# Mixture-of-depths behind ABC attention: row sums in staggered lanes, v's rows stored twice, softmax by halves, and an order from modelled times

## Chip, core and metric

One core of one Trainium2 chip. The metric is the device time of one execution in microseconds, input and output in the chip's memory; the median of several runs counts.

## The reference, cut to what matters

```python
# q, k, v: (8, 8, 576, 64) batch, head, token, width; phi: (8, 8, 576, 32)
a = softmax(phi, axis=2)                        # over the 576 tokens
k_m = einsum('bhsm,bhsd->bhmd', a, k)
v_m = einsum('bhsm,bhsd->bhmd', a, v)
attn = softmax(q @ k_m.transpose(0, 1, 3, 2) / 8)
x = (attn @ v_m), heads side by side            # (8, 576, 512)
scores = einsum('bsd,d->bs', x, w_gate)
out = x.copy()
for b in range(8):                              # the 128 tokens of highest score
    top = argpartition(-scores[b], 128)[:128]
    h = relu(x[b, top] @ w1)                    # 512 -> 1024
    out[b, top] += sigmoid(scores[b, top]) * (h @ w2)
```

The choice of the 128 tokens hangs on close scores, so the softmax is worked out in pieces with a second, small part, and v and a are split into a rounded part ("hi", fp32r) and what is left ("lo").

## The kernel before

A *pair* is a batch and one of its two groups of four heads (4 x 32 memory slots = 128 partitions). The kernel runs through stages, each written as Python generators that take turns; what a generator issues between two `yield`s stands together on each engine, and each engine works in that order.

- **Softmax** (`softmax`, L191 to L277): one batch at a time, both groups side by side in tiles of 128x1152 (`ph`, `num`, `den`, `rl`, `lin`). VectorE does nearly all passes, ScalarE the linear steps and the exponentials (`act`, L187), GpSimd two additions (L223, L267).
- **`split_v`** (L279): ScalarE rounds v to `vhi`, GpSimd subtracts (L288), and GpSimd stores both parts to the tensor `vparts` in HBM (L291).
- **`keys`** (L297): TensorE transposes a (L306), ScalarE copies it to `aS`, GpSimd takes lo (L312) and stores hi and lo twice each to `aparts` (L316); TensorE sums k into `k_m` (L321) and turns it (L331).
- **`values(st)`** (L337): the row sums v_m of four batches at once, one matmul per token and batch (L363). Each batch has 32 partitions (two copies x two parts x eight heads): `v_rows` holds v's rows, `a_rows` a's rows on the diagonal of heads, zeros elsewhere, so that 32 x 64 of v against 32 x 256 of a gives all eight heads. 18 chunks of 32 tokens; a chunk is loaded by eight DMAs of 128 KB for v (L345, 16 partitions side by side each) and eight of 64 KB for a (L350, every eighth partition), all on SP, into one of two buffers.
- **`attention_and_ffn(b)`**: `centre`, `scores` (q against `kT`, L423; exp), `normal` (L404 to L410), `attend` (L475, L478, the gate's scores on VectorE L459 to L464, the store of x, L486), `rank` (the place of each token by comparing, L499 to L530), `gather` (L537 to L551) and `ffn` (L575 w1, L583 w2, store L590).

The order of the stages:

```python
finish(beside(turns([batch(b) for b in range(half)], 8), chain(...split_v...), 1))
...
finish(beside(beside(turns([batch(b) for b in range(half, B)], 8), sums, 2), splits, 1))
...
finish(beside(turns([attention_and_ffn(b) for b in range(SET)], 14, 3), sums, 1))
finish(sums)
finish(turns([attention_and_ffn(b) for b in range(SET, B)], 14, 3))
```

The first `sums` is `values(0)`, beside the softmax of batches 4 to 7; the second is `values(1)`, beside the attention of batches 0 to 3. Buffers of the softmax are given back before the attention's are taken.

Of the kernel before, what the change touches and what calls it, by code (L numbers as in the profile page):

```python
# [20 lines left out]
P = 128  # L21
NC = 6

# [18 lines left out]
NC_T = 6  # L42
# [3 lines left out]
def kernel(  # L46
# [10 lines left out]
    vparts: bass.AP,  # L57
    aparts: bass.AP,
# [9 lines left out]
    NG = phiT.shape[2]  # L68
# [5 lines left out]
    SET = 4  # L74
    T = 32
    NCH = S // T
    scale = 1.0 / Dh ** 0.5
    out_flat = out.rearrange("b s d -> (b s) d")
    pieces = [(n0, min(2 * P, S - n0)) for n0 in range(0, S, 2 * P)]

    nt = -(-capacity // P)
    ranks = [(t * capacity // nt, (t + 1) * capacity // nt) for t in range(nt)]
    assert all(2 <= r1 - r0 <= P for r0, r1 in ranks) and capacity < S

    const = ctx.enter_context(tc.tile_pool(name="const", bufs=1))
    rows = ctx.enter_context(tc.tile_pool(name="rows", bufs=1))
    accp = ctx.enter_context(tc.tile_pool(name="accp", bufs=1, space=PSUM))
    pss = ctx.enter_context(tc.tile_pool(name="pss", bufs=4, space=PSUM))
    first = ExitStack()
    io = first.enter_context(tc.tile_pool(name="io", bufs=2))  # L90
    ex = first.enter_context(tc.tile_pool(name="ex", bufs=2))

    def bank(shape, dtype=F32, name="bank"):
        return pss.tile(list(shape), dtype, tag="bank", name=name)

    phis, ks, qs, vbs = {}, {}, {}, {}

    def load_phi(b):
        phis[b] = io.tile([P, NG, S], F32, name="ph", bufs=3)
        nc.sync.dma_start(out=phis[b], in_=phiT[b])  # L100

    def load_k(b, g):
        ks[b, g] = io.tile([PT, NC, NPR * Dh], F32, name="kb")
        nc.sync.dma_start(out=ks[b, g], in_=k[b, g])

    def load_v(b, g):
        vbs[b, g] = io.tile([P, S * Dh * NPR // P], F32, name="vb")
        nc.sync.dma_start(out=vbs[b, g], in_=v[b, g])

    def load_q(b, i):  # L110
        n0, n = pieces[i]
        qs[b, i] = step.tile([P, NPR, 2 * P], F32, name="qb", bufs=3)
        nc.sync.dma_start(out=qs[b, i][:, :, :n], in_=qT[b, :, :, n0:n0 + n])

    load_phi(0)
    load_v(0, 0)

    ident = const.tile([P, P], F32, name="ident")
    make_identity(nc, ident)

    v_rows = [rows.tile([P, (T + 1) * Dh], F32R, name=f"v_rows{i}") for i in range(2)]
    a_rows = [rows.tile([P, H, T, M], F32R, name=f"a_rows{i}") for i in range(2)]

    kT = [const.tile([P, P], F32, name=f"kT{i}") for i in range(B)]
    v_m = [const.tile([P, P], F32, name=f"v_m{i}") for i in range(B)]
    zs = [const.tile([P, NG, NPR * Dh], F32, name=f"zs{i}") for i in range(2)]

    wg = const.tile([P, D], F32, name="wg")
    iota_r = const.tile([P, capacity], F32, name="iota_r")
    place = const.tile([P, NT], F32, name="place")  # L130
    later = const.tile([P, S], F32, name="later")
    blocks = const.tile([P, P], F32, name="blocks")
    centre_m = const.tile([P, P], F32, name="centre_m")
    means = const.tile([P, NPR, P], F32, name="means")
# [6 lines left out]
    def zero_rows():
        for t in v_rows + a_rows:
            nc.gpsimd.memset(t.bitcast(F32), 0.0)

    def early_consts():
# [6 lines left out]
        nc.vector.scalar_tensor_tensor(out=centre_m, in0=blocks, scalar=-1.0 / M, in1=ident,  # L152
                                       op0=ALU.mult, op1=ALU.add)

    def late_consts():
        nc.sync.dma_start(out=wg, in_=bass.AP(
            tensor=w_gate.tensor, offset=w_gate.offset,
            ap=[[0, P]] + [list(x) for x in w_gate.ap]))
        for t in zs:
            nc.gpsimd.memset(t, 0.0)  # L160
# [15 lines left out]
    def constant(value):  # L176
        t = const.tile([P, 1], F32, name=f"c{len(biases)}")
        nc.gpsimd.memset(t, value)
        return t

    biases = {}
    Q_SHIFT = (127 - 14) * 2.0 ** 23
    for x in (EXP_P[1] * Y0, EXP_Q[1], SQ_B, 1.0, Y0, Q_SHIFT, Y0_BIAS, 1e-9):
        biases[x] = constant(x)

    def act(dst, src, s=1.0, c=0.0, func=AF.Identity):
        nc.scalar.activation(dst, src, func, bias=biases[c] if c else 0.0, scale=s)  # L187
# [531 lines left out]
```

## Time and profile before

| | us |
|---|---|
| median of 3 runs | 1087.49 (1077.97 to 1087.73) |
| the profiled execution | 1083.98 |
| its span, first to last instruction | 1082.3 |

Busy shares of engines are of the span, or of the stretch that a row names. A DMA share of 1 is all 16 DMA engines at work. PEclk is the granted clock of TensorE as a share of 2.4 GHz. "Idle before" is the time for which an engine had nothing to do ahead of a group of instructions, with what ended it.

### The profile page before, as it was taken

To read this page: it belongs to the slowest core of one execution; us is meant where nothing else is said; L and a number is where in the kernel's file an instruction comes from. 1 tells how busy PE (TensorE), PEld (TensorE's weight loads), DVE (VectorE), ACT (ScalarE), POOL (GpSimd) and SP (SyncE) were. 2 spreads that over 40 slices of the span, in tenths; PEclk is the share of its full clock that TensorE was granted. 3 is DMA by queue.
4 is the path that set the end of the run, shared out by engine and by line. 5 is a ranking of instruction groups with operands and counts; after the bars stand their busy time and mean duration, and the time that the engine had idled before them with its cause. 6 is when DMAs were issued, how large, how long until landed. Compare 5 with 4: busy or idle time off the path is not lost. (4 is left out here: it accounts for less than half of the span.)

```text
span 1082.3 us, 17052 instructions
## 1 busy us (share of the span) xinstructions
PE 545.8 (50%) x7162; PEld 426.8 (39%) x7162; DVE 415.5 (38%) x550; ACT 316.1 (29%) x457; POOL 226.1 (21%) x218
## 2 busy tenths in 40 slices
PE   0001201214444456441212767777879877698876
PEld 0000101113444445431111646665656654466555
DVE  7958598545343410347600022011103421434340
ACT  1425345141223100134310413112224305554410
POOL 8536433262324120121530000000000000000000
PEclk9999999957677778765555887688878888697887
DMA  2366621649889889831349899888931121321010
GB/s 87 133 237 237 182 84 34 168 131 239 231 242 237 208 201 159 189 94 53 104 147 241 140 188 158 145 166 151 166 89 54 59 69 54 97 87 61 29 60 13
DMA packets 54147, 146.70 MB, mean 136 GB/s; under 512 B 16560, under 2 KB 24752, under 8 KB 49456
## 3 DMA queue, kind: packets, MB, share of 16 engines
q1 hardware_dynamic: 43056, 103.59, 42.5%
q0 software_dynamic: 11008, 41.95, 11.8%
q8 instruction: 59, 0.97, 0.4%
q14 instruction: 24, 0.20, 0.1%
HBM read 96.21 MB, written 49.28 MB: 134 GB/s over the span
## 5 line engine op out<-in xcount | busy, mean ns | idle before, releaser
L363 PE MATMUL acc<-a_rows,v_rows 32*128 32x256 f32 x4608 | 210.9, 345 | 214.6 <-DMA a_rows<-aparts 180.8
L363 PEld LDWEIGHTS acc<-a_rows,v_rows 32*128 32x128 f32 x4608 | 194.6, 248 | 233.2 <-issue 166.4
L321 PE MATMUL bank<-kb,aS 96*32 96x64 f32 x768 | 24.1, 296 | 130.2 <-ACT aS L308 119.0
L306 PE MATMUL bank<-ident,ph 128*96 128x128 f32 x96 | 23.4, 400 | 102.8 <-DVE ph L271 95.0
L321 PEld LDWEIGHTS bank<-kb,aS 96*32 96x32 f32 x768 | 18.7, 156 | 137.0 <-ACT aS L308 124.0
L575 PE MATMUL bank<-xeT,w_sb 128*128 128x128 f32 x512 | 69.5, 297 | 1.5 <-ACT xeT L568 1.5
L575 PEld LDWEIGHTS bank<-xeT,w_sb 128*128 128x128 f32 x512 | 65.4, 208 | 7.0 <-issue 4.0
L208 DVE SCALAR_TENSOR_TENSOR ph<-q,ph 128x1152 f32<-128x1152 int16 x16 | 28.3, 1767 | 102.5 <-ACT q L187 102.2
L590 POOL DMA_INDIRECT out<-ye,idx x8 | 8.0, 995 | 285.0 <-DVE more L509 208.3
L459 DVE TENSOR_TENSOR prod<-xj,wg 128x1024 f32<-128x1024 f32 (+1 forms) x24 | 25.1, 1044 | 107.3 <-ACT xj L482 107.2
L410 DVE SCALAR_TENSOR_TENSOR eT<-es,rd 128x512 f32<-128x512 f32 (+1 forms) x24 | 13.4, 559 | 136.6 <-ACT rd L408 136.6
L288 POOL TENSOR_TENSOR vb<-vb,vhi 128x1152 f32<-128x1152 f32 x16 | 44.0, 2752 | 92.3 <-ACT vhi L283 92.3
L583 PE MATMUL bank<-w_sb,hT 128*128 128x512 f32 x128 | 62.7, 626 | 0.0
L475 PE MATMUL bank<-zs,eT 128*128 128x256 f32 (+1 forms) x160 | 58.7, 502 | 0.0
L306 PEld LDWEIGHTS bank<-ident,ph 128*96 128x96 f32 x96 | 16.1, 195 | 106.6 <-DVE ph L271 64.5
L551 POOL DMA_INDIRECT xe<-out,idx x8 | 7.9, 989 | 215.5 <-DMA v_rows<-vparts 143.4
L312 POOL TENSOR_TENSOR alo<-aS,ahi 96x768 f32<-96x768 f32 x16 | 33.1, 2066 | 89.3 <-ACT ahi L310 89.3
L283 ACT ACTIVATE vhi<-vb 128x1152 fp32r<-128x1152 f32 x16 | 18.6, 1160 | 110.5 <-DMA vb<-in_v 78.7
L308 ACT ACTIVATE aS<-bank 96x384 f32<-96x384 f32 x32 | 15.0, 476 | 108.0 <-PE bank L306 107.8
L427 ACT ACTIVATE es<-bank 128x256 f32<-128x256 f32 (+1 forms) x48 | 13.2, 324 | 105.6 <-PE bank L423 105.5
L223 POOL TENSOR_TENSOR den<-den,lin 128x1152 f32<-128x1152 f32 x8 | 25.8, 3230 | 85.2 <-DVE den L222 50.3
L509 DVE SCALAR_TENSOR_TENSOR more<-row,tg,later 128x576 bf16<-128x576 f32 (+4 forms) x40 | 20.4, 546 | 59.9 <-ACT row L503 59.9
(121 smaller groups left out, 989.8 us busy)
## 6 DMA issues: line engine op xcount, KB each, us to landing
v_rows<-vparts SPq DMA_DIRECT2D x288, 128.0 KB, 6.3
a_rows<-aparts SPq DMA_DIRECT2D x288, 64.0 KB, 3.9
vb<-in_v SPq DMA_DIRECT2D x16, 576.0 KB, 4.5
vparts<-vb POOLq DMA_DIRECT2D x16, 576.0 KB, 3.6
vparts<-vhi POOLq DMA_DIRECT2D x16, 576.0 KB, 5.1
kb<-in_k SPq DMA_DIRECT2D x16, 576.0 KB, 5.7
aparts<-alo POOLq DMA_DIRECT2D x32, 288.0 KB, 4.1
aparts<-ahi POOLq DMA_DIRECT2D x32, 288.0 KB, 4.8
```

The lines of the kernel that those rows point to most:

```text
L208: stt(out=r, in0=q, scalar=-ln2, in1=r, op0=ALU.mult, op1=ALU.add)
L223: nc.gpsimd.tensor_add(den, den, lin)
L288: nc.gpsimd.tensor_sub(vb, vb, hi.bitcast(F32))
L306: nc.tensor.transpose(out=tp[:, c], in_=a[:, c0 + c], identity=ident)
L312: nc.gpsimd.tensor_sub(lo, aS, hi.bitcast(F32))
L321: nc.tensor.matmul(out=km[r * M:(r + 1) * M], lhsT=aS[:, r, c], rhs=kb[:, c, r * Dh:(r + 1) * Dh], start=(c == 0), stop=(c == NC - 1), ski ...
L363: nc.tensor.matmul(out=accs[bb][:, :H * M].rearrange("p (h m) -> p h m", m=M), lhsT=vr[p, s * Dh:s * Dh + P], rhs=ar[p, :, s], start=(ch = ...
L459: nc.vector.tensor_mul(prod[:n, :cols], x, wg[:n].unsqueeze(1).to_broadcast([n, cols, D]))
L475: nc.tensor.matmul(out=o[:n, g * NPR * Dh:(g + 1) * NPR * Dh], lhsT=eT[:, g, tok:tok + n], rhs=z[:, g], start=(g == 0), stop=False, skip_g ...
L509: nc.vector.scalar_tensor_tensor(out=more[c][:n], in0=row[:n, c * P:], scalar=tg[:n, c, 1:2], in1=later[:n, :S - c * P], op0=ALU.is_gt, op ...
L575: nc.tensor.matmul(out=ps[:, f, :n], lhsT=w1_sb[:, d, (f0 + f) * P:(f0 + f + 1) * P], rhs=xeT[:, d, :n], start=(d == 0), stop=(d == KD - 1 ...
L583: nc.tensor.matmul(out=ps[:n], lhsT=hT[:, f, :n], rhs=w2_sb[:, f], start=(f == 0), stop=(f == KF - 1))
```

## The change

**Lanes.** The row sums of all batches become one sequence of 99 steps of 16 tokens. Lane g (partitions 32g to 32g+31) takes batch g and then batch g+4, and begins nine steps (144 tokens) behind lane g-1. One, two or three lanes are active in 18 steps each, four in 45. A lane's 32 partitions are two parts of v x two of a x four heads x two head groups; v's row stands in the half of the columns that belongs to its group (zeros in the other), so a matmul is 32 x 128 against 32 x 128 and its 128 output partitions hold both groups.

**Rows.** `v_lanes` holds each part of v twice (four stores of 576 KB a pair instead of two). A step is loaded by two DMAs for v (every second partition of the active lanes, 64 KB per lane) and eight for a (8 KB per lane), given in turn to SP or GpSimd: 501 to SP, 489 to GpSimd. There are three row buffers.

**Softmax by halves.** One pair at a time, tiles of 128x576, two pairs in turn. The additions of L223 and L267 and both subtractions go from GpSimd to VectorE.

**Order by a time model.** Every step of every job says which engine it needs, for how long by the author's figures, and which buffers. `Plan.run` keeps a clock per engine and one for DMA, and again and again issues the step with the earliest modelled start, with a bonus for waiting and a malus by job.

```diff
+LANES, T, LAG = 4, 16, 9
+class Plan:
+    RATE = 300.0
+    BIAS = 0.4
+    AGE = 0.3
+    QUEUES = {"Q": ("SP", "POOL"), "QA": ("SP", "POOL", "ACT")}
...
+                engine = min(self.QUEUES.get(engine, (engine,)), key=lambda x: self.free[x])
+                start = max(ready, self.free[engine])
+                key = start + self.BIAS * job[0] - self.AGE * (start - ready)
+                if best is None or key < best[0]:
+                    best = key, start, job, engine, us, names, kb
...
+            end = start + us
+            self.free[engine] = end
+            job[1] = self.now = end + (0.15 if job[3][0] not in self.QUEUES else -0.65)
+            if kb:
+                self.dma = max(self.dma, end + 1.0) + kb / self.RATE
+                self.now = self.dma + 0.9
...
-        nc.gpsimd.tensor_add(den, den, lin)
+        yield "DVE", 0.76
+        tt(out=den, in0=den, in1=lin, op=ALU.add)
...
-        nc.gpsimd.tensor_add(r, r, dl)
+        tt(out=e, in0=e, in1=dl, op=ALU.add)
...
-        nc.gpsimd.tensor_sub(lo, aS, hi.bitcast(F32))
+            lo, = yield "DVE", 0.95, ("alo",)
+            nc.vector.tensor_sub(lo, aS, hi.bitcast(F32))
...
+    def store_v(b, g, w, src, pool, item):
+        yield "POOL", 1.4, (), 1152
+        for alpha in range(2):
+            r0 = ((b % LANES) * 4 + alpha * 2 + w) * NPR
+            dst = v_lanes[g, r0:r0 + NPR, col(b):col(b) + S]
+            nc.gpsimd.dma_start(out=dst.rearrange("h (j s) d -> j h (s d)", j=P // NPR), in_=src)
...
+    def split(b, g, vb):
+        hi, = yield "ACT", 1.16, ("vhi",)
+        nc.scalar.activation(hi, vb, AF.Copy)
+        yield "DVE", 1.36
+        nc.vector.tensor_sub(vb, vb, hi.bitcast(F32))
...
+    def load_v(j, u, eng):
+        on = active(j)
+        g0, g1 = on[0], on[-1] + 1
+        eng.dma_start(out=turn[j][0].bitcast(F32)[32 * g0 + u:32 * g1:NG, :, u],
+                      in_=v_lanes[u, 16 * g0:16 * g1, j * T:(j + 1) * T])
+    def load_a(j, hs, eng):
...
+            eng.dma_start(
+                out=ar[32 * g0 + r * NG + u:32 * g1:H, r].rearrange("p s m -> p (s m)"),
+                in_=a_lanes[r, u, 4 * g0:4 * g1, j * T:(j + 1) * T].rearrange("i s m -> i (s m)"))
...
+    def sums():
+        for j in range(steps):
+            yield "wait", ("rows", j)
+            on = active(j)
+            for s0 in range(0, T, T // 2):
+                yield "PE", 0.12 * T / 2
+                vr, ar = turn[j]
+                for s in range(s0, s0 + T // 2):
+                    for g in on:
...
+                            out=accs[g][:, x * P:(x + 1) * P].rearrange("p (r m) -> p r m", m=M),
+                            lhsT=vr[p, s].rearrange("p u d -> p (u d)"), rhs=ar[p, :, s],
...
+    plan.add(load_phi(pairs), 0)
+    plan.add(constants(), 1)
+    plan.add(split_v(pairs), 1)
+    plan.add(softmax(pairs[0::2]), 0)
+    plan.add(softmax(pairs[1::2]), 0)
+    plan.add(load_k(pairs), 1)
+    plan.add(keys(pairs), 0)
+    plan.add(load_rows(), 0)
+    plan.add(sums(), 0)
+    plan.add(attention(range(0, B, 2)), 1)
+    plan.add(attention(range(1, B, 2)), 1)
+    plan.add(ffn(range(B)), 2)
+    plan.run()
```

How the order moves, at three places. A row is a line, an operation, what it writes and reads, its size, and a count where it stands several times in a row. First, TensorE where the row sums begin. Before, they follow the keys of batch 3 (L331 turns its k_m), and the four batches of the stage alternate:

```order
L306 MATMUL bank<-ident,ph 96x128 x6
L321 MATMUL bank<-kb,aS 32x64 x24
L331 MATMUL bank<-centre_m,kms 128x128
L363 MATMUL acc_858<-a_rows_86,v_rows_84 128x256
L363 MATMUL acc_859<-a_rows_86,v_rows_84 128x256
L363 MATMUL acc_860<-a_rows_86,v_rows_84 128x256
L363 MATMUL acc_861<-a_rows_86,v_rows_84 128x256
```

Now, the same place: they follow the keys of batch 0 (L413, L426), with the transposes of batch 1 (L395) in between:

```order
L413 MATMUL bank_115<-kb_144,aS_145 32x64 x24
L426 MATMUL bank_116<-centre_m,kms_148 128x128
L525 MATMUL acc_104<-a_rows_109,v_rows_108 128x128 x16
L395 MATMUL bank_117<-ident,ph_120 96x128 x3
L525 MATMUL acc_104<-a_rows_111,v_rows_110 128x128 x8
L395 MATMUL bank_114<-ident,ph_120 96x128 x3
```

The sums begin three batches earlier and run with one lane at first. 1,888 of the 4,608 stand ahead of the last key matmuls (L413) of batch 7, in steps 0 to 42.

Second, TensorE at the last row sums. Before, the transposes of v_m (L374) follow, and the ranking of batch 1 (L520):

```order
L363 MATMUL acc_4179<-a_rows_87,v_rows_85 128x256
L363 MATMUL acc_4180<-a_rows_87,v_rows_85 128x256
L363 MATMUL acc_4181<-a_rows_87,v_rows_85 128x256
L363 MATMUL acc_4182<-a_rows_87,v_rows_85 128x256
L374 MATMUL bank<-ident,turned 128x64 x4
L520 LDWEIGHTS more_7026
L520 MATMUL bank<-ones_113,more_7026 128x1
```

Now, the same place, with the last lane alone (acc_107) between the attention of batch 4 (L650, L653) and an FFN (L761 is its transpose, L540 turns the last v_m):

```order
L525 MATMUL acc_107<-a_rows_111,v_rows_110 128x128 x16
L650 MATMUL bank_115<-z_152,eT_158 64x256 x2
L653 LDWEIGHTS ones_91
L653 MATMUL bank_115<-hb_154,ones_91 64x512
L525 MATMUL acc_107<-a_rows_113,v_rows_112 128x128 x16
L761 MATMUL bank_114<-ident,w_137 128x128 x4
L540 MATMUL bank_117<-ident,turned_151 128x128
L691 MATMUL bank_116<-ident,tg_98 128x128 x4
```

Behind the last sum stand 192 of the 256 matmuls with w1, 48 of 64 with w2, 30 of 80 of L650, 48 of 128 of q against kT, and the ranking and gathering of four batches.

Third, the queues of the row loads. Before, SP alone, at the first chunks of a stage (`v_rows_84` and `v_rows_85` are the two buffers):

```order
L156 DMA wg<-in_w_gate 128x512
L100 DMA ph<-in_phiT 128x1152
L345 DMA v_rows_84<-vparts 16x2048 x8
L350 DMA a_rows_86<-aparts 16x1024 x8
L345 DMA v_rows_85<-vparts 16x2048 x8
L350 DMA a_rows_87<-aparts 16x1024 x8
```

Now, GpSimd where four lanes become active, with the stores of v and a (`vhi`, `vb`, `ahi`, `alo`) between the loads; SP has the other half of each step:

```order
L451 DMA v_lanes<-vhi_143 32x4x1152 x2
L451 DMA v_lanes<-vb_141 32x4x1152 x2
L479 DMA v_rows_112<-v_lanes 48x16x64
L487 DMA a_rows_113<-a_lanes 12x512 x4
L441 DMA a_lanes<-ahi_146 96x4x192 x2
L441 DMA a_lanes<-alo_147 96x4x192 x2
L479 DMA v_rows_108<-v_lanes 64x16x64
L487 DMA a_rows_109<-a_lanes 16x512 x4
```

One load of v and about four of a per step stand on each queue, and GpSimd's stand behind stores that wait for VectorE.

## Rows read from the trace of the kernel before

**Rows 1.** The page's first lines: span, and each engine's busy time, share and instructions

```profile
span 1082.3 us, 17052 instructions
PE 545.8 (50%) x7162; PEld 426.8 (39%) x7162; DVE 415.5 (38%) x550; ACT 316.1 (29%) x457; POOL 226.1 (21%) x218
```

**Rows 2.** Busy time by stage: stretch, length, then each engine, granted clock, DMA share, GB/s

```profile
0.00:62.00 62.00, 0.00 (x0) 0.00 (x0) 50.41 (x31) 20.00 (x19) 39.88 (x40) 1.00 0.34 124
62.00:239.00 177.00, 28.18 (x440) 20.65 (x440) 116.70 (x103) 68.97 (x89) 79.33 (x76) 0.93 0.48 150
239.00:490.00 251.00, 118.93 (x2532) 111.11 (x2532) 92.09 (x79) 51.30 (x65) 61.46 (x49) 0.72 0.83 200
490.00:560.00 70.00, 15.31 (x228) 11.82 (x228) 37.46 (x43) 25.39 (x38) 27.97 (x25) 0.52 0.28 80
560.00:801.00 241.00, 157.91 (x2661) 128.28 (x2665) 29.28 (x71) 44.86 (x70) 2.32 (x4) 0.76 0.87 170
801.00:1083.00 282.00, 225.51 (x1309) 154.94 (x1301) 89.56 (x226) 105.58 (x177) 15.17 (x26) 0.81 0.17 56
```

**Rows 3.** Groups by line: the row sums, busy, mean ns, idle time before, releasers

```profile
L363 PE MATMUL acc<-a_rows,v_rows 32*128 32x256 f32 x4608 | 210.9, 345 | 214.6 <-DMA a_rows<-aparts 180.8 <-DMA v_rows<-vparts 24.6 <-DMA vb<-in_v 7.4
```

**Rows 4.** Timeline of TensorE around 750 us: start, length, instructions

```profile
749.18 1.23 PE L363 MATMUL acc<-a_rows,v_rows 32*128 32x256 f32 x32
750.33 2.05 PE L575 MATMUL bank<-xeT,w_sb 128*128 128x128 f32 x16
752.31 1.23 PE L363 MATMUL acc<-a_rows,v_rows 32*128 32x256 f32 x32
```

**Rows 5.** Timeline of the first 60 us: VectorE and GpSimd

```profile
6.32 15.25 DVE L202 TENSOR_SCALAR ph<-ph,mx 128x576 f32<-128x576 f32 x2
13.91 6.93 POOL L143 MEMSET a_rows<- 128x8192 f32 x1
...
34.55 1.36 DVE L222 SCALAR_TENSOR_TENSOR den<-rl,den 128x1152 f32<-128x1152 f32 x1
...
36.06 3.58 POOL L223 TENSOR_TENSOR den<-den,lin 128x1152 f32<-128x1152 f32 x1 [7.81 <-DVE den L222]
37.21 3.65 DVE L225 SCALAR_TENSOR_TENSOR num<-rl,num 128x1152 f32<-128x1152 f32 x1
...
54.61 0.75 DVE L246 SCALAR_TENSOR_TENSOR ph<-num,two_q 128x576 f32<-128x576 f32 x1
```

**Rows 6.** DMA: bytes in all, and issues by tile, KB each, median us to landing

```profile
DMA packets 54147, 146.70 MB, mean 136 GB/s; under 512 B 16560, under 2 KB 24752, under 8 KB 49456
...
v_rows<-vparts SPq DMA_DIRECT2D x288, 128.0 KB, 6.3
a_rows<-aparts SPq DMA_DIRECT2D x288, 64.0 KB, 3.9
...
vparts<-vb POOLq DMA_DIRECT2D x16, 576.0 KB, 3.6
```

**Rows 7.** Issue of DMAs: SP's a loads, GpSimd's stores (min/median/max), and eight a loads

```profile
L350 SPq DMA_DIRECT2D a_rows<-aparts x288: 471/536/1907, 227.2 to 790.6; - x144
...
L316 POOL DMA_DIRECT2D aparts<-alo x32: 677/677/720, 105.4 to 556.4; - x32
...
602.25 7.06 SPq L350 DMA_DIRECT2D a_rows<-aparts  x8
```

**Rows 8.** Groups of TensorE from 801 us on: busy us, mean ns, idle before

```profile
L575 PE MATMUL bank<-xeT,w_sb 128*128 128x128 f32 x448 | 59.8, 294 | 1.5 <-ACT xeT L568 1.5
L583 PE MATMUL bank<-w_sb,hT 128*128 128x512 f32 x112 | 52.2, 603 | 0.0
L475 PE MATMUL bank<-zs,eT 128*128 128x256 f32 (+1 forms) x120 | 44.6, 509 | 0.0
```

More of the change, by code (lines that the diff above doesn't have):

```diff
@@ L1 @@
 from contextlib import ExitStack
-from itertools import chain
 import concourse.bass as bass
@@ L73 @@
     KD, KF = D // P, F // P
-    SET = 4
-    T = 32
-    NCH = S // T
+    half = S // 2
     scale = 1.0 / Dh ** 0.5
     out_flat = out.rearrange("b s d -> (b s) d")
[L79 to L86, printed above, removed]
@@ L141, in zero_rows, with sb, several @@
[L141 to L145, printed above, removed]
+    per = S // T
+    steps = (B // LANES) * per + (LANES - 1) * LAG
+    assert capacity <= P and capacity < S and S % T == 0
+    mem = ctx.enter_context(tc.tile_pool(name="mem", bufs=1))
+    psum = ctx.enter_context(tc.tile_pool(name="psum", bufs=1, space=PSUM))
+    def sb(shape, dtype=F32, name="sb"):
+        return mem.tile(list(shape), dtype, name=name)
+    def several(n, shape, dtype=F32, name="sb"):
+        return [sb(shape, dtype, f"{name}{i}") for i in range(n)]
@@ new lines, in load_k, with softmax, chain_of @@
+    def load_k(pairs):
+        for b, g in pairs:
+            yield "wait", ("half", b, g)
+            kb, = yield "SP", 0.6, ("kb",), 576
+            ks[b, g] = kb
+            nc.sync.dma_start(out=kb, in_=k[b, g])
+            signal(("k", b, g))
+    def softmax(pairs):
+        for b, g in pairs:
+            yield "wait", ("phi", b, g)
+            yield from chain_of(b, g)
+    def chain_of(b, g):
+        r = phis.pop((b, g))
+        sm, i16 = yield "DVE", 1.31, ("sm", "i")
+        mx, den_s, rcp, top, low = (sm[:, x:x + 1] for x in range(5))
+        q, rh = i16[:, 0], i16[:, 1]
+        nc.vector.tensor_reduce(mx, r, axis=AX.X, op=ALU.max)
+        signal(("begun", b, g))
+        yield "DVE", 0.46
+        nc.vector.tensor_scalar(out=r, in0=r, scalar1=mx, scalar2=EXP_LOWEST,
+                                op0=ALU.subtract, op1=ALU.max)
+        yield "ACT", 0.65
@@ L615, in turns @@
-    def turns(jobs, lag, width=2):
-        jobs, live, since = list(jobs), [], lag
-        while jobs or live:
-            if jobs and len(live) < width and since >= lag:
-                live.append(jobs.pop(0))
-                since = 0
-            since += 1
-            for job in list(live):
-                if next(job, live) is live:
-                    live.remove(job)
-                else:
-                    yield
-    def beside(main, other, n):
-        for _ in main:
-            for _ in range(n):
-                next(other, None)
-            yield
@@ L636, in batch @@
-    def batch(b):
-        if b + 1 < B:
-            load_phi(b + 1)
-        yield from softmax(b)
-    early_consts()
-    zero_rows()
-    half = B // 2
-    finish(beside(turns([batch(b) for b in range(half)], 8),
-                  chain(*[split_v(b) for b in range(half)]), 1))
-    splits = chain(*[split_v(b) for b in range(half, B)])
-    late_consts()
-    sums = values(0)
-    finish(beside(beside(turns([batch(b) for b in range(half, B)], 8), sums, 2), splits, 1))
-    finish(splits)
@@ L664 @@
-    sums = values(1)
-    finish(beside(turns([attention_and_ffn(b) for b in range(SET)], 14, 3), sums, 1))
-    finish(sums)
-    finish(turns([attention_and_ffn(b) for b in range(SET, B)], 14, 3))
-    ps = bank([1, B, len(pieces)])
-    nc.tensor.matmul(out=ps.rearrange("p b i -> p (b i)"), lhsT=ones,
-                     rhs=good.rearrange("p b i -> p (b i)"), start=True, stop=True)
-    sums_ok = work.tile([1, B, len(pieces)], F32, name="sums_ok")
-    for i, (n0, n) in enumerate(pieces):
-        nc.vector.tensor_single_scalar(sums_ok[:, :, i], ps[:, :, i], H * n - 0.5, op=ALU.is_gt)
```

988 lines of the change are left out of this document (556 added, 432 removed).

## The prediction

> **What bounds the kernel now.** I read the page's shares first: TensorE is busy half of the 1082.3 us span and no engine more [rows 1]. So the time is lost between engines, and the table by stage says where [rows 2]. From 0 to 239 us VectorE is busy 50.4 and 116.7 us, TensorE hardly: softmax of four batches. From 239 to 490 us the row sums of batches 0 to 3 run beside the second softmax, and the DMA share is 0.83. From 490 to 560 us the rest of that softmax runs nearly alone. From 560 to 801 us the sums of batches 4 to 7 run beside the first attentions, DMA share 0.87, TensorE busy 158 of 241 us. From 801 us TensorE is busy 225.5 of 282 us and the DMA share is 0.17. The bound changes four times. That DMA is the limit of the two row stages is seen at the sums' own line: 214.6 us of idle time ahead of it, 180.8 of them ended by a landing of a_rows [rows 3].
>
> **The change, part by part.** The stages become one program, and its engine orders have three stretches. I price each by the resource that ends it.
>
> *DMA.* The kernel moves 146.7 MB today; 288 loads of 128 KB (37.7 MB) and 288 of 64 KB (18.9 MB) are rows [rows 6]. v's two parts are stored twice now, another 32 stores of 576 KB, 18.9 MB, so 165.6 MB. At what rate? Outside the row stages a full share is worth 56/0.17 = 329 GB/s (801 to 1083 us) [rows 2]. The stage from 560 us moved 170 GB/s x 241 us = 41.0 MB in 0.87 x 241 = 210 us of full share; 28.3 MB were rows, the other 12.7 MB at 329 take 39 us, so the rows ran at 28.3/171 = 165 GB/s. A v load filled 16 partitions side by side; now it takes every second partition of all lanes. No row shows that form: its bounds are 165 and 329 GB/s. I take 329 for v, whose spread over the partitions now resembles the other tiles' loads, and 165 for a, whose loads shrink.
>
> *VectorE.* Four jobs leave GpSimd for it (the two subtractions, the two softmax additions). A pass over half the columns takes 0.75 us (L246), a whole undisturbed one 1.36 us (L222) [rows 5]. A half needs 20 passes (15.0 us), v's subtraction at 1.36, a's (96x768, between these two) at 0.93, a maximum and a clamp (0.7 and 0.5) and small ones (0.9): about 19.5 us, 16 times is 312 us. What it gets in return: beside a GpSimd addition a VectorE pass took 3.65 us instead of 1.36, and two clamps took 15.25 us beside the clearing of a_rows [rows 5]. GpSimd has no such work after its start now.
>
> *Row sums.* 4,608 matmuls stay, but 128 columns wide instead of 256, because two head groups share the 128 output partitions. Warm, 32 of the old ones lie 1.15 us apart from the next piece (749.18 to 750.33), so four lanes' step costs 144 ns [rows 4]. Where columns alone decide it falls to 72, where weights or issue decide it stays 144. I take 110 ns per token step, between the ends because the trace does not separate weights from columns, and give steps with fewer than four lanes the same price. The Trainium skill (TensorE: Matmul & The Clock Gate, "Wait - 56ns, not 53.3ns?") says that starts of matmuls never come closer than about 25 ns, however narrow. By that rule 2,720 sums of the second stretch take an estimated 68 us instead of my 99, and the time would be some 40 us shorter; no run here shows it yet.
>
> *First stretch, to the last keys.* 1,888 of the 4,608 sums (41%) stand ahead of the last key matmuls on TensorE. So DMA moves phi, k, v (23.5 MB), the stores (56.6 MB), the weights (4.4 MB) and 41% of the rows (23.2 MB: 15.5 of v, 7.7 of a). That is 84.5/329 = 257 us, 47 us and 47 us: 351 us. The row stages never passed a share of 0.87 [rows 2], so 351/0.87 = 403 us. VectorE needs 312/0.92 + 22 us to begin = 361 us, less; GpSimd and SP issue some 630 and 610 DMAs in all, at 0.68 and 0.54 us [rows 7] nowhere near. I take 405; ends are 361 (VectorE alone) and 457 (all rows at 165).
>
> *Second stretch, to the last sum.* Attention work on TensorE: from 801 us seven FFNs ran (448 of 512 and 112 of 128 records), 59.8 + 52.2 us, 16.0 each, and six attentions (120 of 160 records) [rows 8]. The rest, 225.5 - 112.0 us over six, is 18.9 each. Eight of both are 279 us. Behind the last sum the order leaves 192 of 256 w1 matmuls, 48 of 64 w2 and 30 of 80 of attention with the ranking of a fourth batch: 6 x 16.0 + 3.3 x 18.9 = 158 us. About 14 us lie ahead of the last keys. So 107 us are left here, and 56 of the 99 steps, 896 token steps at 110 ns = 99 us. 206 us at a busy share of 225.5/282 = 0.80 [rows 2] are 257 us. DMA has 22.3/329 + 11.1/165 + 15/329 = 181 us, over 0.87 208 us: covered by TensorE. This is what is late next once the row loads no longer are. Ends: 208, and (107 + 129)/0.66 = 358 with the share of 560 to 801 us.
>
> *Third stretch.* 158/0.80 = 198 us; with shares of 0.9 and 0.7, 176 and 226.
>
> *Sum.* 405 + 257 + 198 = 860 us of span; 1.7 us lie around the span in the profiled run (1083.98 against 1082.3), and the median is 3.5 us above it: **865 us**. The granted clock (0.76 and 0.81 of 2.4 GHz in the last two stages, a mixture of the two levels) is in these rows and taken as it is.
>
> *Waits added.* SP and GpSimd serve row loads, input loads, stores and outputs in one order each. A store of v that waits for VectorE's subtraction holds back half of the next step's rows on GpSimd; three row buffers stand against that. I cost it inside the 0.87 and 0.80.
>
> **The rivals.**
>
> *Denser than I think.* An order by modelled times could keep every stretch's bound 90% busy: 361, (107 + 82)/0.9 = 210, 176: about 750 us. For it: VectorE lost much to GpSimd. Against: no stage reached 0.9.
>
> *The order binds.* If real times leave the planned ones, every engine waits at its head. Then softmax keeps today's pace (239 us for four batches, 478 for eight), the second stretch today's 0.66 (312 us), the third 0.70 (226 us): about 1015 us.
>
> *The rows stay packed*, all at 165 GB/s: 457 us, then (33.4/165 + 15/329)/0.87 = 285, then 198: 940 us.
>
> *Slower: row loads cost by the piece.* There are 990 instead of 576, 10 per step, and an a load shrinks from 64 to at most 32 KB. In one stretch eight a loads took 7.06 us, 0.88 each [rows 7]. If both queues together can do no better, a step takes 8.8 us, 99 take 871; with 62 us ahead and 198 behind that is 1131 us. It decides from 8.4 us per step. Against: their issue alone takes 0.54 us (median) and landing 3.9 us [rows 6, 7], so several are in flight and they stood behind packed v loads. The Trainium skill (DMA: Bandwidth & Descriptors, "Rules for kernel authors") speaks for this rival: under 64 KB a transfer is mostly overhead and should be joined to others. The trace agrees only in part, since loads of 64 KB overlap one another here.
>
> *It does not do what it says:* lanes of one width give no overlap between row groups. Then a sum costs 128 ns like a full f32 matmul (16 in 2.05 us, L575) [rows 4]; the second stretch is (107 + 348)/0.80 = 569 us, in all 1172 us. Against: today's sums overlap, at 36 ns each.
>
> **How the numbers follow.** Forecast 0.57; denser 0.18; the order binds 0.10; packed rows 0.05; by the piece 0.06; no overlap 0.04. Low is the denser rival's 750, also the sum of all low ends (361 + 208 + 176 = 745). High is 1010, near the binding order; the sum of all high ends is 1041. About 1% is what a measurement tells from no change. The first four cases are all faster, less a little for a binding order that eats everything: 0.89 faster, 0.02 the same, 0.09 slower.
>
> **What would show it.** Right: the last key transposes near 405 us; VectorE passes of half width at 0.75 us throughout; token steps of four lanes at 110 ns; the last sum near 660 us with TensorE then 80% busy for some 200 us; row loads no longer the releaser of most idle time ahead of the sums. Wrong: a DMA share above 0.8 up to the last sum (packed or by the piece), TensorE waiting for rows with DMA half idle (the order, or issue), sums at 128 ns each.

## The result and the profile after

| | before | after |
|---|---|---|
| median of 4 runs | 1085.95 us | 867.08 us (862.65 to 877.22) |
| ratio, 95% interval | | 0.7982 [0.792, 0.8044] |
| the profiled execution | 1083.98 | 865.3 |
| its span | 1082.3 | 863.5 |

Forecast were 865 us. The median hits it to 2 us, and the three stretches tell how far that was insight. The first ends with the last key matmul (L413), the second with the last row sum (L525):

| stretch of the program | before | predicted | after |
|---|---|---|---|
| to the last key matmul | 545 | 405 | 365 |
| from there to the last row sum | 256 | 257 | 297 |
| the rest | 281 | 198 | 201.5 |
| span | 1082 | 860 | 863.5 |

Two errors of 40 us cancel, so that the hit is this close is luck. Of the 219 us gained, 180 come from the first stretch and 80 from the third; the second gives 41 back. Of the four executions of e5, e6 and e9 below, three each are more than 1.5% slower than the fastest one; e5 and e6 have no ratio for that, and e9's goes by the median of all four.

First the page's head, to be set beside [rows 1]; after the shares stand the granted clock in 40 slices of the span and the DMA line that answers to the first of [rows 6]:

```profile
span 863.5 us, 18155 instructions
...
PE 655.9 (76%) x6994; PEld 524.9 (61%) x6994; DVE 422.9 (49%) x837; ACT 313.4 (36%) x505; POOL 384.0 (44%) x680
...
PEclk9999999999999999955569697797555979797777
...
DMA packets 140972, 165.68 MB, mean 192 GB/s; under 512 B 93664, under 2 KB 101856, under 8 KB 140880
```

TensorE is busy 656 us where it was 546, for 168 matmuls fewer: its records have become longer, not more. The bytes are the 165.6 MB forecast. Next the table by stretch, with the columns of [rows 2]; the second row is the dense part of the first:

```profile
0.00:365.00 365.00, 212.36 (x2756) 186.85 (x2756) 299.15 (x499) 192.48 (x297) 210.17 (x378) 1.00 0.93 298
...
75.00:365.00 290.00, 205.26 (x2646) 181.50 (x2646) 230.59 (x391) 150.71 (x237) 174.17 (x317) 1.00 0.97 301
...
365.00:662.00 297.00, 292.71 (x3409) 232.57 (x3400) 70.63 (x189) 67.23 (x117) 162.84 (x291) 0.69 0.59 162
662.00:863.00 201.00, 150.79 (x840) 105.52 (x839) 53.15 (x151) 53.72 (x91) 10.95 (x11) 0.83 0.14 45
```

The first two stretches have one full resource each now. Up to 365 us DMA is full (0.97 from 75 us on). From 365 to 662 us TensorE is: 292.7 of 297 us. From 662 us nothing is full, and TensorE is busy three quarters. The row sums' part of TensorE (first columns) in the first two stretches:

```profile
0.00:365.00 365.00, 152.43 (x1824) 143.23 (x1824) 1.00 0.93 298
365.00:662.00 297.00, 168.51 (x2784) 155.60 (x2784) 0.69 0.59 162
```

And their group, first on the page, to be set beside [rows 3], then from 365 to 662 us alone:

```profile
L525 PE MATMUL acc<-a_rows,v_rows 32*128 32x128 f32 x4608 | 321.2, 364 | 99.2 <-DMA a_rows<-a_lanes 92.2
...
L525 PE MATMUL acc<-a_rows,v_rows 32*128 32x128 f32 x2784 | 168.7, 340 | 3.2 <-DMA a_rows<-a_lanes 2.8 <-issue 0.3
```

Idle time ahead of the sums fell from 214.6 to 99.2 us. A landing of a_rows still ends nearly all of it, but 96 of the 99 us lie in the first stretch, where DMA is full. Pieces of TensorE's timeline (start, length, instructions) give the price of a token step, from the start of one row to the start of the next:

```profile
326.30 3.68 PE L525 MATMUL acc<-a_rows,v_rows 32*128 32x128 f32 x64 [5.44 <-DMA a_rows<-a_lanes]
...
354.41 1.12 PE L525 MATMUL acc<-a_rows,v_rows 32*128 32x128 f32 x32
355.46 0.59 PE L395 MATMUL bank<-ident,ph 128*96 128x128 f32 x3
...
404.85 3.68 PE L525 MATMUL acc<-a_rows,v_rows 32*128 32x128 f32 x64
408.46 0.80 PE L731 MATMUL bank<-tg,pick 128*128 128x2 f32 x3
...
471.27 1.11 PE L525 MATMUL acc<-a_rows,v_rows 32*128 32x128 f32 x32
472.31 0.74 PE L713 MATMUL bank<-ones,more 128*128 128x1 bf16 x15
...
646.89 3.67 PE L525 MATMUL acc<-a_rows,v_rows 32*128 32x128 f32 x16
650.49 2.08 PE L650 MATMUL bank<-z,eT 128*128 128x256 f32 x4
```

From 471.27 to 472.31 us eight token steps of four lanes take 1.04 us, 130 ns each. At 404.85 sixteen take 3.61 us, 226 ns each. At 646.89 sixteen steps of the last lane alone take 3.60 us, 225 ns each: one lane costs as much as four. What lies between 130 and 226 is in the clock column of the same table, by shorter stretches:

```profile
375.00:440.00 65.00, 64.17 (x838) 53.64 (x836) 11.84 (x36) 14.78 (x26) 34.69 (x63) 0.50 0.66 185
...
450.00:480.00 30.00, 30.00 (x582) 25.51 (x584) 11.49 (x34) 8.53 (x14) 19.94 (x36) 1.00 0.79 217
...
550.00:590.00 40.00, 39.71 (x514) 33.07 (x512) 13.83 (x37) 11.29 (x20) 27.67 (x50) 1.00 0.58 151
...
600.00:662.00 62.00, 62.00 (x220) 44.25 (x218) 10.83 (x22) 8.98 (x15) 20.92 (x38) 0.50 0.24 70
```

TensorE stood at its lower level, 1.2 GHz, from 375 to 440 and from 600 to 662 us while it was busy 99% of the time. Its clock rose in the ten microseconds from 440, where the first FFN (L776) joins sums and attention. The 1.00 that the column shows all the way to 365 us can't be taken for the clock there. The 64 sums at 326.30 us last as long as those at 404.85 us, at the lower level, and in the run with 64 columns below the same place reads 0.5 with the same times; the 32 sums at 354.41 us take 1.05 us, as at the upper level. Where column and durations differ, the durations tell the level.

### The profile page after: what moved, and what is told of

It reads as the page before. It is cut to its first block, busy times and chain, and to the rows that moved or that the text cites. A ratio compares the mean times of both kernels' runs of the same rounds, so it can differ in the third digit from the quotient of the medians.

```text
span 863.5 us, 18155 instructions
## 1 busy us (share of the span) xinstructions
PE 655.9 (76%) x6994; PEld 524.9 (61%) x6994; DVE 422.9 (49%) x837; ACT 313.4 (36%) x505; POOL 384.0 (44%) x680
## 5 line engine op out<-in xcount | busy, mean ns | idle before, releaser
L525 PE MATMUL acc<-a_rows,v_rows 32*128 32x128 f32 x4608 | 321.2, 364 | 99.2 <-DMA a_rows<-a_lanes 92.2
L525 PEld LDWEIGHTS acc<-a_rows,v_rows 32*128 32x128 f32 x4608 | 298.9, 274 | 144.0 <-issue 81.8
L487 POOL DMA_DIRECT2D a_rows<-a_lanes x391 | 196.4, 508 | 47.5 <-DMA v_lanes<-vb 13.9
L479 POOL DMA_DIRECT2D v_rows<-v_lanes x98 | 74.9, 764 | 155.0 <-PE acc L525 120.0
L776 PE MATMUL bank<-w,w_sb 128*128 128x128 f32 x512 | 76.0, 308 | 2.2 <-ACT w L765 2.2
L776 PEld LDWEIGHTS bank<-w,w_sb 128*128 128x128 f32 x512 | 70.1, 218 | 8.4 <-ACT w L765 3.4
L792 PE MATMUL bank<-w_sb,w 128*128 128x512 f32 x128 | 70.9, 678 | 0.0
L395 PE MATMUL bank<-ident,ph 128*96 128x128 f32 x96 | 27.0, 425 | 45.1 <-DVE ph L373 45.1
L650 PE MATMUL bank<-z,eT 128*128 128x256 f32 (+1 forms) x160 | 53.7, 467 | 0.0
L395 PEld LDWEIGHTS bank<-ident,ph 128*96 128x96 f32 x96 | 15.5, 195 | 48.6 <-issue 42.1
L229 ACT ACTIVATE w<-i,c 128x576 f32<-128x576 int16 (+1 forms) x48 | 36.1, 764 | 16.9 <-DVE w L334 16.0
L650 PEld LDWEIGHTS bank<-z,eT 128*128 128x128 f32 (+1 forms) x160 | 30.9, 214 | 9.6 <-issue 2.7
L761 PE MATMUL bank<-ident,w 128*128 128x128 f32 x32 | 8.9, 433 | 32.7 <-DMA w<-out,idx 32.7
```

What stands on the lines that cost most here:

```text
L395: nc.tensor.transpose(out=tp[:, c], in_=a[:, c0 + c], identity=ident)
L479: eng.dma_start(out=turn[j][0].bitcast(F32)[32 * g0 + u:32 * g1:NG, :, u], in_=v_lanes[u, 16 * g0:16 * g1, j * T:(j + 1) * T])
L487: eng.dma_start(out=ar[32 * g0 + r * NG + u:32 * g1:H, r].rearrange("p s m -> p (s m)"), in_=a_lanes[r, u, 4 * g0:4 * g1, j * T:(j + 1) * ...
L525: nc.tensor.matmul(out=accs[g][:, x * P:(x + 1) * P].rearrange("p (r m) -> p r m", m=M), lhsT=vr[p, s].rearrange("p u d -> p (u d)"), rhs= ...
L650: nc.tensor.matmul(out=o[:n, g * NPR * Dh:(g + 1) * NPR * Dh], lhsT=eT[:, g, c * P:c * P + n], rhs=z[:, g], start=(g == 0), stop=False, sk ...
L776: nc.tensor.matmul(out=bank[:, f * P:f * P + n], lhsT=w1_sb[:, d, (f0 + f) * P:(f0 + f + 1) * P], rhs=xeT[:, d * P:d * P + n], start=(d == 0),
```

## The experiments

The runs that follow are compared by the same three cuts: the last keys, the last row sum, the end.

**Half the token steps** (e1). This and the runs that leave work out name in their expectation what is left out.

```diff
-                for s in range(s0, s0 + T // 2):
+                for s in range(s0, s0 + T // 2, 2):
```

> Every second token is left out of the row sums (2,304 matmuls instead of 4,608); order, loads and stores stay. Theory (TensorE sets the second stretch, DMA the first): the sums behind the last keys took 168.7 us, half of them goes, so the second stretch falls from 297 to about 215 us, the first stays at 365 us, the span is about 780 us. Rival (rows set the second stretch, by their bytes or by the piece, and TensorE only looks busy): nothing moves by more than 10 us, span 855 to 865 us.

Measured: 841.85 us in one run, span 840.0, cuts at 373 and 639.3 us. The table by stretch, from the first cut to the second:

```profile
373.00:639.30 266.30, 254.58 (x2019) 184.81 (x2012) 67.66 (x183) 67.26 (x117) 161.80 (x289) 0.59 0.64 178
```

The sums alone in that stretch:

```profile
373.00:639.30 266.30, 108.70 (x1391) 94.53 (x1392) 0.59 0.64 178
```

Half the sums are gone, and the stretch is 31 us shorter. Neither number was met. That TensorE is the bound holds (96% busy), but what is left costs more: the sums 108.7 us over 456 token steps, 238 ns each instead of 185, the other work 146 us instead of 124. The granted clock fell from 0.69 to 0.59. That is not all of it, since 238 ns are more than the 226 of the lower level. The pieces are half as long here, and a short piece costs more per step:

```profile
409.20 3.68 PE L525 MATMUL acc<-a_rows,v_rows 32*128 32x128 f32 x64
412.81 1.21 PE L590 MATMUL bank<-qb,kT 64*32 64x288 f32 x16
...
418.10 1.12 PE L525 MATMUL acc<-a_rows,v_rows 32*128 32x128 f32 x16
419.15 1.11 PE L761 MATMUL bank<-ident,w 128*128 128x128 f32 x4
```

Sixteen token steps in one piece take 3.61 us, 226 ns each; four take 1.05 us, 262 ns each. So half the sums are not half the price, and the 31 us are less than half of what the sums cost.

**v stored and loaded once** (e2).

```diff
-        for alpha in range(2):
+        for alpha in range(1):
...
-                      in_=v_lanes[u, 16 * g0:16 * g1, j * T:(j + 1) * T])
+                      in_=v_lanes[u, 8 * g0:8 * g1, j * T:(j + 1) * T])
```

> The second copy of v's rows is neither stored nor loaded (every fourth partition instead of every second; the others keep zeros), so half of the products of the row sums is left out; instructions and order stay, 37.8 MB less of DMA, 26.6 MB of it ahead of the last keys. Theory (DMA sets the first stretch, at 0.97 of its share and 301 GB/s): 26.6 MB less let VectorE bind, 299 us of work at 0.92 to 0.95 and 20 us to begin, so the last keys come near 335 to 345 us instead of 365, the rest stays, span 835 to 845 us. Rival (VectorE and the order set the first stretch already): last keys at 360 to 365 us, span 860 us.

Measured: 843.78 us in one run, span 842.1, by stretch:

```profile
0.00:345.00 345.00, 211.35 (x2740) 185.91 (x2744) 298.25 (x498) 190.86 (x297) 192.42 (x350) 1.00 0.76 238
345.00:636.00 291.00, 285.65 (x3430) 226.85 (x3418) 69.97 (x187) 67.58 (x118) 155.74 (x288) 0.71 0.47 126
```

As expected: the first stretch loses 20 us and the second 6. With the DMA share at 0.76 the first stretch is no longer held by DMA. VectorE, busy 298 of 345 us, was close behind it.

**Sums of 64 columns** (e3); half the memory slots are left out.

```diff
-                            lhsT=vr[p, s].rearrange("p u d -> p (u d)"), rhs=ar[p, :, s],
+                            lhsT=vr[p, s].rearrange("p u d -> p (u d)"), rhs=ar[p, :NPR if n + s == 0 else NPR // 2, s],
```

> All row sums but each batch's first are 64 columns wide instead of 128, so half of the products are left out; count, order, loads and stores stay. Theory (a token step costs its weight loads or its issue, not its columns): four lanes still take about 130 ns warm and 225 ns at the low clock, span within 1% of 863.5 us. Rival (columns decide): a step falls by a third or more, the second stretch by 50 us or more, span below 815 us.

Measured: 902.04 us in one run, span 900.3, cuts at 368.3 and 701.3 us: 35 us longer, which neither theory had. The stretch between the cuts:

```profile
368.30:701.30 333.00, 330.38 (x3412) 265.76 (x3404) 68.81 (x186) 67.35 (x117) 162.54 (x291) 0.59 0.52 144
```

TensorE's timeline at the place where after has its 64 sums of 326.30 us:

```profile
326.15 3.63 PE L525 MATMUL acc<-a_rows,v_rows 32*128 32x64 f32 x64 [4.46 <-DMA a_rows<-a_lanes]
```

At the lower level 64 sums last 3.63 us where those of 128 columns last 3.68: columns don't price a step there. And the clock is lower for longer, 0.59 where the same stretch of after has 0.69 (the 0.72 of the next expectation is that of 365 to 700 us). So the next run went the other way.

**Sums of 256 columns** (e9): a's row is streamed twice into two halves of the bank, one of which is read. Twice the columns, the same result.

```diff
-                            lhsT=vr[p, s].rearrange("p u d -> p (u d)"), rhs=ar[p, :, s],
+                            lhsT=vr[p, s].rearrange("p u d -> p (u d)"), rhs=ar[p, :, s].unsqueeze(1).to_broadcast([32, 2, NPR, M]),
```

> Every row sum is 256 columns wide again: the same 128 of a are streamed twice, into the two halves of the lane's bank, and the second half is not read; count, order, loads and stores stay. Theory (what the sums cost is the granted clock, and narrower sums lowered it: 64 columns gave 0.59 in the second stretch where 128 gave 0.72): wider sums hold the clock higher, a four-lane step costs about 145 ns warm instead of 225 ns cold, the attention beside it gets faster too, the second stretch falls from 297 to 240 to 270 us, time 820 to 845 us. Rival (work is work: 128 more columns a matmul are 53 ns at 2.4 GHz and 107 at 1.2): a step costs 20 to 100 ns more, the second stretch grows by 15 to 60 us, time 880 to 930 us.

Measured: median 845.66 us (825.59 to 853.99), ratio 0.7782 [0.7728, 0.7835]; the profiled run is the fastest, 825.59, with cuts at 367.3 and 623.3 us. The stretch between them, all of it:

```profile
367.30:623.30 256.00, 241.51 (x3417) 188.53 (x3407) 69.64 (x185) 67.39 (x118) 163.94 (x292) 0.91 0.68 188
```

Its sums alone:

```profile
367.30:623.30 256.00, 141.73 (x2783) 124.08 (x2784) 0.91 0.68 188
```

And TensorE's timeline where the clock is 1.00:

```profile
470.15 1.23 PE L525 MATMUL acc<-a_rows,v_rows 32*128 32x256 f32 x32
471.31 0.72 PE L590 MATMUL bank<-qb,kT 64*32 64x288 f32 x16
```

A step at the upper level costs 145 ns (1.16 us for eight), 15 more than with 128 columns, and yet the stretch is 41 us shorter, at a granted clock of 0.91. By the medians the kernel is 21 us faster, and all four runs (825.59 to 853.99) lie below all four of after (862.65 to 877.22). The stretch came as theory had it, the median a little above its 845. In the first stretch, which DMA holds, nothing changed. In one table (sums behind the first cut, over 912 token steps):

| run | columns | granted clock | ns per step |
|---|---|---|---|
| e3 | 64 | 0.59 | 205 |
| after | 128 | 0.69 | 185 |
| e9 | 256 | 0.91 | 155 |

The same order of instructions stands in all three, so the width is what differs. Why the clock differs with it isn't shown. Each row is one profiled run, e9's its fastest, and e9's runs spread over 28 us, so the 41 us are its best case.

**No overlap of sums and attention** (e7).

```diff
-                yield "wait", ("vm", b)
+                for bb in range(B):
+                    yield "wait", ("vm", bb)
```

> Every batch's attention waits in the planner until all row sums are done; the rest of the change stays, so this takes out the overlap of sums and attention alone. Theory (TensorE is full in the second stretch, so overlap there saves only what attention alone leaves idle): the second stretch holds 2,784 sums at the low clock, some 200 us, the third all of the attention, 279 us of work at a busy share of 0.75 to 0.80, 350 to 370 us; time 905 to 945 us. Rival (the overlap is the main gain of the change): 1000 us or more. Second rival (it gains nothing): within 1.5% of 867 us.

Measured: median 907.52 us (906.44 to 912.21), ratio 0.8369 [0.8313, 0.8425]. By stretch, from the first cut on:

```profile
369.00:586.00 217.00, 205.09 (x2797) 199.16 (x2792) 0.00 (x0) 3.82 (x14) 153.68 (x280) 1.00 0.65 166
586.00:907.00 321.00, 256.03 (x1500) 173.15 (x1499) 124.16 (x347) 127.90 (x210) 16.14 (x16) 0.88 0.21 69
```

538 us behind the first cut instead of 498: the overlap is worth 40 us, as theory had it. The sums alone take 201 us in the first of these rows, 221 ns per step, the price of the lower level, though the column says 1.00.

**Four jobs, on GpSimd and on VectorE** (e4 gives the two additions and two subtractions back to GpSimd inside the new program; e8 gives them to VectorE in the program before). One line of four:

```diff
-        yield "DVE", 0.76
-        tt(out=den, in0=den, in1=lin, op=ALU.add)
+        yield "POOL", 1.6
+        nc.gpsimd.tensor_add(den, den, lin)
```

> The four element jobs (two subtractions, two softmax additions) go back to GpSimd, inside the new order. Theory (moving them is a needed part: GpSimd now issues half of the row loads and all stores): its 174 us of work between 75 and 365 us grow by some 124 us and VectorE passes beside them slow from 0.75 to 2 us, so the last keys come near 440 us and the time is 920 to 950 us. Rival (the first stretch is DMA's alone, the jobs are a side matter): within 1.5% of 867 us.

> The kernel before, with one part of the change alone: its four element jobs on VectorE instead of GpSimd. Theory (that part pays only with the rest): GpSimd's 124 us become some 58 us of VectorE passes, about 45 us of slowed passes come back, and the two softmax additions take 1.4 instead of 2.6 to 3.2 us of the chain; the stages ended by DMA and by TensorE stay, ratio to before 0.975 to 1.0. Rival (contention between the two engines was the main loss of before): the first 239 us shrink by 50 us or more, ratio 0.95 or less.

Measured: e4 median 945.7 us (942.27 to 992.4), ratio 0.8705 [0.8629, 0.8782]; e8 1068.1 us (1064.79 to 1069.77), ratio 0.9825 [0.9792, 0.9858]. e4 by stretch:

```profile
0.00:398.50 398.50, 194.50 (x2454) 175.30 (x2455) 334.51 (x430) 182.36 (x282) 293.79 (x373) 1.00 0.84 263
398.50:736.00 337.50, 332.54 (x3733) 262.81 (x3725) 74.74 (x206) 79.27 (x136) 173.54 (x309) 0.85 0.55 153
```

One line of VectorE, in after and in e4 (min/median/max in ns, first and last start):

```profile
L332 DVE SCALAR_TENSOR_TENSOR w<-w,w x16: 757/758/759, 20.4 to 306.5; 128x576 f32<-128x576 f32 x16
...
L332 DVE SCALAR_TENSOR_TENSOR w<-w,w x16: 757/1844/5501, 22.7 to 342.6; 128x576 f32<-128x576 f32 x16
```

Both totals were met. The same four jobs are worth 18 us in the old program and 79 in the new one. VectorE has 64 instructions fewer than in after and is busy 35 us longer in the first stretch, because its passes stretch beside GpSimd's (median 1844 ns here, 758 in after). The first cut comes 33 us late, not the 75 expected; the rest is the second stretch, where TensorE is full and has 256 sums (1,568 instead of 1,824 stand ahead of the last keys) and some 70 other matmuls more to do. Its 0.85 is no better clock than after's 0.69: up to 530 us the column reads 1.00 over 1,340 sums that take 59 ns each, as at the lower level (the sums in the first column):

```profile
398.50:530.00 131.50, 79.19 (x1340) 74.96 (x1344) 0.55 (x2) 1.00 0.66 184
```

**FFN first** (e6) and **a lag of five** (e5).

```diff
-    plan.add(ffn(range(B)), 2)
+    plan.add(ffn(range(B)), 0)
```

```diff
-LANES, T, LAG = 4, 16, 9
+LANES, T, LAG = 4, 16, 5
```

> The FFN's jobs get the best place in the planner (0 instead of 2), nothing else changes; only the order moves. Theory (TensorE sets the second and third stretch, and the clock was granted in full once w1 and w2 matmuls stood between the sums, from 444 us): FFN work moves from the third into the second stretch, where it lifts the clock; the third shrinks by more than the second grows, time 825 to 855 us. Rival (TensorE is full there, so work only changes places): within 1.5% of 867 us.

> The lanes stand 80 tokens apart instead of 144, so 87 steps instead of 99 and 10 instead of 18 each with one, two or three lanes; work, bytes and columns stay. Theory (a token step costs the same for one lane as for four, about 225 ns at the low clock): 12 steps of 16 tokens less, some of them in the first stretch where TensorE has room; 20 to 40 us less, partly given back since the last four batches end closer together, time 835 to 865 us. Rival (a step costs by its matmuls): no gain from steps, and the bunched end makes the third stretch longer by 20 us or more, time 880 us or more.

Measured: e6 median 837.49 us (818.19 to 838.86), as theory had it. e5 891.68 (844.37 to 913.52), which settles nothing; the profiled run is its slowest. The stretch between the cuts of e6:

```profile
375.70:689.70 314.00, 311.78 (x3630) 245.24 (x3622) 76.50 (x212) 76.17 (x133) 161.12 (x283) 0.78 0.54 155
```

And of e5:

```profile
354.00:685.00 331.00, 325.86 (x3392) 263.62 (x3384) 53.93 (x145) 63.53 (x110) 148.72 (x264) 0.51 0.50 142
```

FFN matmuls among the sums lengthen this stretch by 17 us, at a clock of 0.78, and shorten the rest from 201 to 145. In this run of e5 TensorE is 98% busy and stays at its lower level for nearly the whole stretch.

**v's rows packed** (e12): each part of v into 16 partitions side by side, one DMA per lane, 576 v loads of 64 KB instead of 198 of 64 to 256 KB; the rows' parts then meet others than they should.

```diff
-        eng.dma_start(out=turn[j][0].bitcast(F32)[32 * g0 + u:32 * g1:NG, :, u],
-                      in_=v_lanes[u, 16 * g0:16 * g1, j * T:(j + 1) * T])
+        for g in on:
+            eng.dma_start(out=turn[j][0].bitcast(F32)[32 * g + 16 * u:32 * g + 16 * u + 16, :, u],
+                          in_=v_lanes[u, 16 * g:16 * g + 16, j * T:(j + 1) * T])
```

> v's rows are loaded to 16 partitions side by side, one DMA for each active lane and head group (two to eight a step, 64 KB each) instead of two DMAs over every second partition of all lanes; the same bytes, and the planner's order stays. The rows then stand against the wrong rows of a, so the sums are other sums, of the same shape. Theory (the spread over the partitions lifted v's rows from 165 to some 310 GB/s): 15.5 MB ahead of the last keys take about 45 us more, the last keys come near 405 to 415 us, the second stretch, TensorE's, grows by less, time 900 to 930 us. Rival (the rate comes from elsewhere, the spread is a side matter): the last keys stay at 365 to 375 us, time within 1.5% of 867 us.

Measured: median 966.8 us (959.14 to 973.21), ratio 0.8909 [0.8839, 0.8979], cuts at 411.4 and 765.9 us. By stretch:

```profile
75.00:411.00 336.00, 221.21 (x2626) 194.64 (x2630) 232.06 (x390) 151.29 (x237) 212.12 (x398) 1.00 0.92 261
411.00:766.00 355.00, 344.77 (x3432) 275.29 (x3424) 70.51 (x189) 67.47 (x117) 218.29 (x403) 0.70 0.55 135
```

The w1 matmuls in the second stretch, in after and in e12 (busy us, mean ns, idle before), and e12's sums alone up to 490 us (first column):

```profile
L776 PE MATMUL bank<-w,w_sb 128*128 128x128 f32 x128 | 19.2, 296 | 0.0
...
L777 PE MATMUL bank<-w,w_sb 128*128 128x128 f32 x128 | 27.4, 381 | 0.0
...
411.00:490.00 79.00, 49.01 (x832) 46.60 (x832) 0.55 (x2) 1.00 0.78 188
```

The direction is as expected, the size larger. The first stretch is 46 us longer: 261/0.92 = 284 GB/s per full share against 301/0.97 = 310. By estimate that rate is 27 of the 46 us (87.3 MB at either rate, at a share of 0.97), and the share of 0.92 the rest. The 378 more issues are part of it and weren't tried apart. Another 58 us are TensorE's, busy 345 us in its stretch where it was 293: as many records, each longer, the w1 matmuls 381 ns on average instead of 296, so a lower clock again. The 0.70 in its row hides this, since the column reads 1.00 up to 490 us, where the sums take 59 ns each, as at the lower level. Why packed rows should lower TensorE's clock isn't shown.

**Wide sums and FFN first, without and with a lag of five** (e10, e11): the edits of e9, e6 and e5 together.

> 256 columns and the FFN first in the planner, both at once. Theory (both act on the granted clock and on the idle time of the third stretch, by different means): clock above 0.9 up to the last sum, time 790 to 815 us. Rival (each takes the same loss away): 820 to 845 us, no better than either alone.

> As the one before, and the lanes 80 tokens apart instead of 144. Theory (with the clock held, 12 steps of 16 tokens at some 145 ns less are 28 us, of which the bunched end gives back 10 to 20): 780 to 810 us, at or a little below the run without it. Rival (the smaller lag itself lowers the clock or lengthens the third stretch, as its run at 128 columns may be read): 15 us or more above it.

Measured: e10 median 813.56 us (809.94 to 814.83), ratio 0.7484 [0.7437, 0.7532]; e11 810.95 us (800.95 to 817.06), ratio 0.7419 [0.7346, 0.7491]. Of e10 the stretch from its first cut to its second:

```profile
364.90:668.20 303.30, 286.24 (x3634) 220.38 (x3622) 77.26 (x213) 75.89 (x134) 165.77 (x291) 0.91 0.59 165
```

Theory's clock and time came, the rival's 820 to 845 us did not, and e10 beats both kernels, by 54 us the new one. Whether the two gains add up is open: by the medians 21 and 30 us stand against 54, by the fastest run of each 37 and 44 against 53. What the shorter lag adds to e10 isn't told apart from none.

## Why the prediction was right, and where it only seemed so

**What bounds it.** DMA first, TensorE next: the forecast's chain holds. e2 shows the first half (less DMA, 20 us earlier keys), the TensorE column of the second stretch with e1 and e9 the other. Of the signs that the prediction named, the VectorE passes of 0.75 us came, and the last sum near 660 us, but by the two errors. The last keys (365, not 405 us) and the token step (185, not 110 ns) did not; a_rows still ends 92 of the 99 us of idle time ahead of the sums; TensorE was then 75% busy where 80% were said.

**First stretch, 40 us too long.** The bytes were right: 298 GB/s over 365 us are 108.8 MB, 107.7 were counted. Full share time was near too: 108.8 MB at 298/0.93 = 320 GB/s is 340 us, I had 351. The step that failed is "so 351/0.87": a cap of 0.87 read from the old row stages, with one queue and two buffers. With 10 loads per step from two queues into three buffers the share is 0.97 from 75 us on; which of these lifts it wasn't tried. The 165 GB/s for a's rows did not fall: the second stretch moved 162 GB/s x 297 us = 48.1 MB in 0.59 x 297 = 175 us of full share, where 48.4 MB in 181 us were counted with it.

**VectorE.** Half passes take 0.76 us (758 ns median at L332), where 0.75 were forecast, and it is busy 299 us of the first stretch where 312 were counted for the softmax.

**Second stretch, 40 us too short.** The step that failed is "I take 110 ns per token step". It cost 185 ns (168.5 us over 912 steps; 1,824 sums lay ahead of the last keys, 64 fewer than I counted), 70 us more than the 99 forecast. Both of my ends, 72 and 144, came from one row at the upper clock [rows 4], while this stretch ran at 0.69. At the upper level the step took 130 ns, near the end at which columns don't decide. That steps of fewer lanes cost the same was right (225 and 226 ns). The other work took 124 us instead of 107. Together 293 us instead of 206, and at the forecast's 0.80 that would have been 366. But TensorE was busy 0.986 of the time, so it became 297. The share erred in the kernel's favour, by luck and not by reckoning: the order has attention work between the sums, and idle time ahead of the sums is 3.2 us here.

The Trainium skill (TensorE: Matmul & The Clock Gate, "Wait — 56ns, not 53.3ns?") gives a floor of about 25 ns between the starts of matmuls; taken as a price, it would have put the estimate another 40 us lower. Here that floor wasn't reached: the sums of four row groups came 32.5 ns apart at the upper level (1.04 us for 32) and 56 at the lower (3.61 us for 64).

**Third stretch.** 158 us of work were forecast and 150.8 measured, at a share of 0.75 instead of 0.80: 201.5 against 198 us.

**The rivals.** *Denser* got its share right in the second stretch and its sums wrong. *The order binds* fell: 3.2 us of idle ahead of the sums there. *The rows stay packed* fell. Packing v again (e12) cost 46 us in the first stretch, near the 52 (457 to 405) forecast for it, but with 378 more issues. In the second the rival had 28 us more (285 to 257), for DMA, where e12 lost 58 us on TensorE. *By the piece* fell: 792 of the 990 row loads are of 32 KB or less, and DMA still moved 301 GB/s. The Trainium skill (DMA: Bandwidth & Descriptors, "Rules for kernel authors") stood on this rival's side, with mostly overhead under 64 KB. GpSimd's largest loads land after 4.5 and 4.0 us, as the next rows show (KB each, median us to landing), but enough are in flight that this time isn't paid in turn.

```profile
v_rows<-v_lanes POOLq DMA_DIRECT2D x45, 256.0 KB, 4.5
...
a_rows<-a_lanes POOLq DMA_DIRECT2D x182, 32.0 KB, 4.0
```

*No overlap between row groups* fell too: 32.5 ns a sum, not 128.

**Where the 219 us come from.** The runs price parts of it, not as a sum, since each was undone alone: the four jobs 79 us (e4), sums beside attention 40 us (e7), v's spread 46 us of the first stretch (e12, 100 us in all); v's second copy costs about 23 (867.08 to 843.78, one run). The narrowing of the sums is no part of the gain: with 256 columns again the kernel is 21 us faster (e9). That the softmax by halves, the earlier start of the sums or the modelled order as such is worth the rest wasn't tried.

## What to carry to other kernels

Price TensorE work at the clock that its own stretch will have: the same step cost 1.7 times as much at the lower level (226 against 130 ns), and a busy share of 0.99 did not keep the clock up here. When two limits alternate, interleave the stages and then ask which resource is full in each stretch: edits to that one moved the time (e2 in the first, e9 in the second). Ask also which one is close behind, since it takes over (VectorE in e2, and in e4, where slower passes made the first stretch 33 us longer at a DMA share of 0.84). Check a hit by its stretches, since errors of 40 us can cancel in the total.

## What was not expected of the hardware

- With the order of instructions unchanged, sums of 64, 128 and 256 columns ran at mean granted clocks of 0.59, 0.69 and 0.91 in the second stretch, and the widest were the fastest (333, 297, 256 us; one profiled run each, the last the fastest of four).
- TensorE stayed at 1.2 GHz for 65 us on end while busy 99%, and for 331 us at a mean of 0.51 in the slowest run with a lag of five, at 98%.
- At the lower level a step of one lane costs 225 ns and of four lanes 226: lanes that are not active save nothing. A piece of four steps costs 262 ns a step, one of sixteen 226.
- A clock column of 1.00 can stand where the sums' own durations are those of the lower level: in after at 326 us, in e7 from 369 to 586 us (221 ns a step).
